# Attention and a two-layer MLP on one core: seven products for half of the first layer of four more token groups, and q and k of ten sets turned by a DMA

## The chip, the cores and the metric

The kernel runs on one core of one Trainium2 chip. The metric is the device time of one execution in microseconds; smaller is better. The kernel before takes 321.13 us, the median of three runs (320.48, 321.13 and 321.16).

## The reference: what is computed

Eight batches with eight heads, 576 positions of 64 elements per head, and 16 "beacon" positions ahead of the keys and values of each head. First causal attention (the beacons are seen by every query), then a two-layer MLP over the 4608 tokens of 512 elements, with an inner dimension of 2048. All inputs and the output are float32.

```python
k_all = concat([beacon_k, k], axis=2); v_all = concat([beacon_v, v], axis=2)   # 592 keys
scores = matmul(q, k_all^T) / sqrt(64);  scores above the diagonal (keys after the beacons) = -1e9
a = softmax(scores);  x = matmul(a, v_all) -> transposed to (4608, 512)
h = x @ w_in                       # 512 -> 2048
g = h * sigmoid(1.702 * h)
out = g @ w_out                    # 2048 -> 512
```

## The kernel before, in words

**Tiles and stages.** The work is done in float16 with sums in float32. Attention is cut into 16 *sets* of four heads of one batch (two sets per batch). Sets 0 to 3 are "early" and computed in finer pieces while the loads of the start come in. Scores are made transposed (keys on partitions, queries along the columns), with only the blocks below the diagonal: 1664 columns per head and set. From set 4 on these columns are laid end to end over all sets and cut into *chunks* of 512 columns; a chunk fills one score buffer `s` of four PSUM banks, one for each head, and can hold the end of one set and the beginning of the next. There are 55 chunks, numbered from 0; chunk 16 is the first of set 4. For each chunk PE computes the scores (`e_qk`, L506), ACT takes the exponential (`e_exp`, L518) into `E`, and POOL sets the part above the diagonal to zero (`e_mask`, L536). When a set is complete, DVE adds up pieces for the row sums (`e_zadd`, L554), PE multiplies by v (`e_av`, L594), and DVE inverts the row sums and writes the normalised result (`e_norm`, L628) into `xT`, a ring of 4 x 576 = 2304 tokens, in the layout that the MLP reads.

**How q and k come in.** POOL issues one DMA for q and one for k of each set (`e_load_qk`, L416), which casts to float16 and puts 18 consecutive positions of a head on one partition (long runs in DRAM). There are three buffers for each (`NB3` = 3). DVE then turns each of the two with a transpose of 32x32 blocks (`e_turn`, L472; for k also a small one for the beacons, L465, after a cast, L457, out of `bkf`, in which all sets' beacon keys lie). The result has 32 partitions for each head, and two elements of a head's 64 beside each other in a column, so that the scores of a piece take two matmuls of 32 rows (`d` = 0, 1) for each of four heads, the four heads in four row groups of the array. The turned q and k have two buffers each (`NB2` = 2): the turn of set s waits for the last scores of set s-2.

**The MLP.** The tokens are cut into groups: 0 and 1 have 256 tokens, 2 to 9 have 512. Numbers of groups here are the program's, from 0; the "token groups 4 to 7" of the change are 3 to 6. Groups 0 and 1 go a plain way. For groups 2 to 9 the second layer is done by seven products of half-sized blocks instead of eight (`products`, `e_prod`, L770), with sums of the activations before (`e_s`, L718, into three buffers `sA`), sums of w_out made once (`e_t`), and joins afterwards on DVE (`e_join`, L786, out of PSUM into `osb`, four buffers); SP stores the result (`e_store4`, L794). For groups 7, 8 and 9 (`FAST`) the first layer is done by seven products too: `fast` works in four *fours* of a group, each of two tiles of either half of the inner dimension; `e_part` (L864) does one product as four matmuls of 256 columns. ACT copies a partial result to another bank (`e_seed`, L874, two per four) and one product to SBUF (`e_keep7`, L883), DVE adds that back in (`e_sum7`, L886, two per four), and ACT applies the gelu (`e_gelu4`, L892). It needs four sums of the tokens per group (`e_xs`, L718 under `add`) and four sums of w_in (`e_ws`), which lie in q and k buffers that are no longer needed. For groups 2 to 6 the first layer is plain: 16 tiles of four matmuls with 512 columns (`e_m1`, L652), then gelu on ACT (`e_gelu`, L674). A group that crosses a multiple of 2304, which is group 5, has its 512 columns cut in two of 256.

**PSUM.** Eight banks: four (`RING`) for the MLP and the values, four for the score buffer. After the last chunk (`plan.breaks`) the score banks join the ring.

**ACT's tables.** Exponential and gelu need different tables; a change of table costs a table load, which the profile shows as ACT_TABLE_LOAD. Copies (`nc.scalar.mul`) need none.

**What sets the order.** The program first builds a list of operations with durations, due times and dependences (`Plan`, `op`), and places them on the engines in the order that the literal lists `ORDER` give for PE, ACT, DVE, POOL, Q (the landing of POOL's DMAs) and SP. The durations in the plan only serve to choose buffers and to merge the lists into one program; on the chip each engine runs its own list strictly in order and waits on semaphores.

Of the kernel before, what the change touches and what calls it, by code (L numbers as in the profile page):

```python
# [7 lines left out]
F16 = mybir.dt.float16  # L8
# [37 lines left out]
    ],  # L46
    "ACT": [
# [13 lines left out]
    ],  # L61
    "DVE": [
# [44 lines left out]
    ],  # L107
}


HELD = ("s", "zadd", "xsum", "wsum", "t", "mask", "bk")

# [1340 lines left out]
```

## Time and profile before

| | |
|---|---|
| median of three runs | 321.13 us (320.48 to 321.16) |
| span of the profiled execution, first to last instruction | 319.1 us |
| PE busy, of the span | 312.4 us (98%) |
| DVE busy | 246.5 us (77%) |
| ACT busy | 220.0 us (69%) |
| POOL busy | 113.2 us (35%) |
| bytes moved by DMA | 28.80 MB in 58379 packets, of which 41312 under 512 B |

The page names no other time of the profiled execution than its span. PE, DVE, ACT, POOL and SP are the engines; PEld is the loading of weights into the array, which overlaps with PE. L506 is line 506 of the kernel before; out<-in are names of the program's tiles. The shares of the page are averages over a start that waits for loads, a long middle and a short end; where a step matters, it is read from the stretch in which it lies.

### The profile page before, as it was taken

How to read it: one execution, taken by the hardware profiler on the slowest of the kernel's cores; microseconds unless marked ns; L12 is line 12 of the kernel's file. 1: busy time of each engine (PE TensorE's matmuls, PEld its weight loads, DVE VectorE, ACT ScalarE, POOL GpSimd, SP SyncE). 2: the span in 40 equal slices, each digit the busy share in tenths (PEclk: the TensorE clock that was granted, in tenths of full speed). 3: DMA queues.
4: the chain of work that ended last, by engine and by line, in shares of the span. 5: the costliest groups of instructions: out<-in, count | busy, mean ns of one | idle time of the engine just before them, and what ended most of it. 6: DMA issues, size and time to landing. Idle time of an engine off the chain costs nothing.

```text
span 319.1 us, 9554 instructions
## 1 busy us (share of the span) xinstructions
PE 312.4 (98%) x4119; PEld 223.9 (70%) x4119; DVE 246.5 (77%) x484; ACT 220.0 (69%) x275; POOL 113.2 (35%) x178
## 2 busy tenths in 40 slices
PE   6999999999999999999999999999999999999995
PEld 2567855544875467754778877646788888888884
DVE  4769966896797778875788979888978975684773
ACT  1777986557767686698867685778779786666520
POOL 8768488670238413472084108420420000000000
PEclk9999999999999999999999999999999999999999
DMA  7999999993109911398085707710021000011112
GB/s 122 175 202 209 206 192 185 170 228 65 37 2 165 208 26 37 46 153 123 7 81 90 115 2 81 100 35 2 2 83 51 4 20 15 33 69 36 67 68 99
DMA packets 58379, 28.80 MB, mean 90 GB/s; under 512 B 41312, under 2 KB 53728, under 8 KB 58336
## 3 DMA queue, kind: packets, MB, share of 16 engines
q0 software_dynamic: 47552, 18.49, 49.0%
q1 hardware_dynamic: 10576, 9.63, 9.3%
q8 instruction: 32, 0.52, 0.7%
q14 instruction: 11, 0.09, 0.1%
q10 hardware_dynamic: 208, 0.07, 0.1%
HBM read 37.22 MB, written 9.44 MB: 146 GB/s over the span
## 4 chain that ended last, share of the span: by engine, by line
PE 89%; DMA 5%; POOL 2%; ACT 1%; DVE 1%; issue 0%; DVEq 0%; POOLq 0%
PE u L770 31%; PE u L652 25%; PE u L864 12%; PE u L594 9%; PE s L506 8%; PE u L698 5%; DMA kn<-in_k_dram 3%; DMA qn<-in_q_dram 2%; POOL w L438 1%; ACT E L518 1%; ACT L674 0%; DVE kT L472 0%; POOL qn L416 0%; POOL kn L416 0%; ACT g L674 0%
## 5 line engine op out<-in xcount | busy, mean ns | idle before, releaser
L518 ACT ACTIVATE E<-s 128x2048 f16<-128x2048 f32 (+3 forms) x59 | 90.7, 1552 | 35.4 <-PE s L506 32.5
L652 PE MATMUL u<-xT,w 128*128 128x256 f16 (+1 forms) x512 | 87.9, 326 | 0.1
L536 POOL TENSOR_SCALAR_AFFINE_SELECT E<-E 128x512 f16<-128x512 f16 (+3 forms) x78 | 48.7, 643 | 89.6 <-ACT E L518 89.5
L652 PEld LDWEIGHTS <-w 128*128 128x128 f16 x512 | 49.2, 98 | 32.8 <-issue 1.1
L674 ACT ACTIVATE g<-u 128x512 f16<-128x512 f32 x80 | 43.6, 598 | 15.9 <-PE u L652 15.6
L770 PEld LDWEIGHTS <-g 128*128 128x128 f16 x512 | 48.4, 98 | 7.6 <-issue 0.5
L786 DVE SCALAR_TENSOR_TENSOR osb<-u,osb 128x512 f32<-128x512 f32 (+2 forms) x51 | 33.2, 654 | 21.5 <-PE u L770 16.3
L770 PE MATMUL u<-w,g 128*128 128x256 f16 x384 | 49.7, 273 | 0.0
L770 PEld LDWEIGHTS <-sA 128*128 128x128 f16 x384 | 36.6, 98 | 6.0 <-issue 0.8
L892 ACT ACTIVATE g<-u 128x512 f16<-128x512 f32 x48 | 27.2, 602 | 14.0 <-PE u L864 8.6
L506 PEld LDWEIGHTS <-kT 32*128 32x128 f16 x1088 | 22.4, 92 | 17.5 <-issue 10.8
L770 PE MATMUL u<-tB,sA 128*128 128x256 f16 x256 | 34.2, 273 | 0.0
L628 DVE TENSOR_TENSOR xT<-u,rz 128x352 f16<-128x352 f32 (+2 forms) x52 | 26.1, 521 | 8.4 <-PE u L594 7.7
L506 PE MATMUL s<-qT,kT 32*128 32x192 f16 (+14 forms) x992 | 30.9, 247 | 0.5 <-ACT E L518 0.3
L432 POOL DMA_DIRECT2D vb<-in_v_dram x32 | 27.8, 873 | 3.1 <-PE u L594 1.4
L594 PE MATMUL u<-E,vb 128*32 128x352 f16 (+8 forms) x928 | 27.7, 262 | 0.1
L594 PEld LDWEIGHTS <-vb 128*32 128x32 f16 (+1 forms) x928 | 20.1, 96 | 6.7 <-issue 2.9
L554 DVE TENSOR_TENSOR zs<-zs,E 128x1344 f16<-128x1344 f16 (+2 forms) x36 | 21.8, 605 | 0.9
L472 DVE STREAM_TRANSPOSE kT<-kn 128x576 f32<-128x576 f32 x16 | 20.1, 1256 | 2.7 <-DMA kn<-in_k_dram 2.2
L718 DVE TENSOR_TENSOR sA<-g 128x512 f16<-128x512 f16 x32 | 13.2, 417 | 10.9 <-ACT g L674 10.7
L472 DVE STREAM_TRANSPOSE qT<-qn 128x576 f32<-128x576 f32 x16 | 19.8, 1240 | 0.8 <-DMA qn<-in_q_dram 0.7
L864 PEld LDWEIGHTS <-w 128*128 128x128 f16 x192 | 18.7, 98 | 2.3
(76 smaller groups left out, 401.1 us busy)
## 6 DMA issues: line engine op xcount, KB each, us to landing
out_dram<-osb SPq DMA_DIRECT2D x35, 256.0 KB, 2.6
kn<-in_k_dram POOLq DMA_DIRECT2D x16, 288.0 KB, 6.8
qn<-in_q_dram POOLq DMA_DIRECT2D x16, 288.0 KB, 6.4
vb<-in_v_dram POOLq DMA_DIRECT2D x24, 128.0 KB, 6.8
w<-in_moe_w_in_dram POOLq DMA_DIRECT2D x8, 256.0 KB, 9.4
w<-in_moe_w_out_dram POOLq DMA_DIRECT2D x4, 512.0 KB, 12.1
vb<-in_v_dram POOLq DMA_DIRECT2D x8, 112.0 KB, 6.0
vb<-in_v_dram POOLq DMA_DIRECT2D x8, 80.0 KB, 6.8
```

The lines of the kernel that those rows point to most:

```text
L432: nc.gpsimd.dma_start(out=t[0 : hi - lo, j, h0:h1, :], in_=v[b, h0:h1, lo:hi, :].rearrange("h n d -> n h d"),)
L472: nc.vector.transpose(out=f32(dst.rearrange("p n e -> p (n e)")).rearrange("p (r t) -> p t r", t=TR), in_=f32(src[:, :]).rearrange("p (t c ...
L506: nc.tensor.matmul(u[:, o : o + w], kT[s % NB2][r : r + 32, j * P : (j + 1) * P, d], qT[s % NB2][r : r + 32, a : a + w, d], start=(d == 0) ...
L518: nc.scalar.activation(out=Es[s][:, h0:h1, c0:c1], in_=sall[(i, p)][:, :, o : o + c1 - c0], func=AFT.Exp, scale=0.125,)
L536: nc.gpsimd.affine_select(out=blk, in_=blk, compare_op=ALU.is_ge, fill=0.0, base=off + (Nb if j == 0 else 0), pattern=[[0, Q], [1, w]], ch ...
L594: nc.tensor.matmul(u[32 * h : 32 * h + 32, a:e], lhs, src[0:kw, h, col : col + e - a], start=first, stop=last, skip_group_check=s >= EARLY ...
L652: nc.tensor.matmul(u[:, o + a - t0 : o + e - t0], w1t[:, kp, nt * P : (nt + 1) * P], xT[:, kp, a % XR : (e - 1) % XR + 1], start=(kp == 0 ...
L674: nc.scalar.activation(out=gts[g][:, n0:n1, 0:w], in_=rings[("m1", g, n0)][:, 0 : n * w].rearrange("p (n w) -> p n w", n=n), func=AFT.Gelu ...
L770: nc.tensor.matmul(u[:, HM * mt : HM * (mt + 1)], lhs[:, n, mt * P : (mt + 1) * P], rhs[:, n, :], start=(n == 0 and (mt == 0 or apart) and ...
L786: nc.vector.scalar_tensor_tensor(out=osbs[(g, dst)][:, c0:c1], in0=rings[("p", g, p)][:, c0:c1], scalar=scale_of(g), in1=osbs[(g, src)][:, ...
L864: nc.tensor.matmul(u[:, HM * n : HM * (n + 1)], lhs[x][:, (2 * i + n) * P : (2 * i + n + 1) * P], rhs[:, x, :], start=fresh and n == 0 and ...
L892: nc.scalar.activation(out=gts[g][:, n : n + 2, HM * h : HM * (h + 1)], in_=rings[src][:, :].rearrange("p (n w) -> p n w", n=2), func=AFT. ...
```

## The change: what it does

1. **First layer.** `FAST` is now a table: groups 3 to 6 do the first two of their four fours by seven products and the other two plainly; groups 7 to 9 all four as before; group 2 none, but goes through the same function. For groups 2 to 6 the first layer is bound to a place after a given chunk (`PHASE`): there the four score banks join the ring, and the scores of the next chunk wait until all gelus of the group are done.
2. **Buffers for it.** The sums of w_in get tiles of their own (`SF`), the fourth sum of tokens as well (`ST[3]`); the kept product goes to four slots in the old q and k buffers, once sets 0 to 5 are turned. `sA` shrinks from three buffers to one: two of the sums are written over their inputs, and so wait for the product that reads these.
3. **Ring of tokens.** 2048 tokens instead of 2304. No group crosses its end any more; a normalised result that does is written in two instructions.
4. **q and k of sets 6 to 15.** POOL copies q, k and the beacons' k from DRAM to DRAM into scratch tensors with the cast to float16 (`e_stage`: rows of positions, four heads of 64 elements beside each other). SP then issues one transposing DMA for k and one for q (`e_xbar`) out of the scratch into the turned buffers, after the staging has landed and the scores two sets earlier are done. A head now lies on 64 partitions, and the scores of a piece are four matmuls of 64 rows in two row groups. Sets 0 to 5 keep the old way, with two load buffers instead of three, and `bkf` holds only their beacons.
5. **Order.** All lists of `ORDER` are new, and a list `BANK` gives the PSUM bank of each tile.

```diff
-    NE, NB2, NB3 = 3, 2, 3
+    NE, NB2, NB3 = 3, 2, 2
...
-    XR = 4 * S
+    XR = 2048
...
-    sA = [cst.tile([P, HN, HM], F16, tag=f"sA{i}", name=f"sA{i}") for i in range(3)]
+    sA = cst.tile([P, HN, HM], F16, tag="sA", name="sA")
+    SF = {i: cst.tile([P, 2, DFF // 2], F16, tag=f"SF{i}", name=f"SF{i}") for i in range(1, 5)}
...
-    bkf = cst.tile([P, NSET, D], F32, tag="bkf", name="bkf")
+    SQR = 3 * HS
+    bkf = cst.tile([P, SQR, D], F32, tag="bkf", name="bkf")
...
+    x7 = [f32(t[:, 0 : 2 * 512]) for t in qn + kn]
+    qD = [dr.tile([S, Q * D], F16, tag=f"qD{s}", name=f"qD{s}") for s in range(SQR, NSET)]
+    kD = [dr.tile([NK, Q * D], F16, tag=f"kD{s}", name=f"kD{s}") for s in range(SQR, NSET)]
+    qP, kP = ([t[:, :].rearrange("p (c n) -> p c n", c=2) for t in x] for x in (qTt, kTt))
...
+    def e_stage(s, which):
+        b, hs = divmod(s, HS)
+        hh = slice(Q * hs, Q * hs + Q)
+        if which == 2:
+            dst, src = kD[s - SQR][0:Nb, :], beacon_k[b, hh]
+        elif which:
+            dst, src = kD[s - SQR][Nb:NK, :], k[b, hh]
+        else:
+            dst, src = qD[s - SQR][:, :], q[b, hh]
+        nc.gpsimd.dma_start(out=dst.rearrange("n (h d) -> n h d", h=Q), in_=src.rearrange("h n d -> n h d"))
+
+    def e_xbar(s, which):
+        src, dst = ((qD, qP), (kD, kP))[which]
+        nc.sync.dma_start_transpose(out=dst[s % NB2][:, :, 0 : NK if which else S], in_=src[s - SQR][:, :])
...
+            if s >= SQR:
+                for h, u in heads.items():
+                    r = D * (h % 2)
+                    nc.tensor.matmul(
+                        u[:, o : o + w],
+                        kP[s % NB2][r : r + D, h // 2, j * P : (j + 1) * P],
+                        qP[s % NB2][r : r + D, h // 2, a : a + w],
+                        start=True,
+                        stop=True,
+                    )
+                continue
...
         if i == 0:
             add(eng, s1, a21, a22, ALU.add)
         elif i == 1:
-            add(eng, s2, s1, a11, ALU.subtract)
+            add(eng, a11, s1, a11, ALU.subtract)
         elif i == 2:
-            add(eng, s4, a12, s2, ALU.subtract)
+            add(eng, a12, a12, a11, ALU.subtract)
...
-    FAST = (7, 8, 9)
-    PHASE = {}
-    plan.breaks = sorted(set(PHASE.values())) + [len(CHUNKS) - 1]
+    FAST = {2: (), 3: (0, 1), 4: (0, 1), 5: (0, 1), 6: (0, 1), 7: (0, 1, 2, 3), 8: (0, 1, 2, 3), 9: (0, 1, 2, 3)}
+    PHASE = {2: 19, 3: 27, 4: 35, 5: 41, 6: 48}
+    plan.breaks = sorted(PHASE[g] for g in FAST if g in PHASE) + [len(CHUNKS) - 1]
...
+    XBAR = 1800
...
+            for which in (2, 1, 0) if s >= SQR else (1, 0):
+                if s >= SQR:
+                    staged[(s, which)] = pool_load(
+                        560 if which == 2 else 1300, 200 if which == 2 else 2000, [], lambda s=s, which=which: e_stage(s, which),
+                        name=f"st{s}.{which}.",
+                    )
...
     def turns(s):
+        if s >= SQR:
+            for which in (1, 0):
+                turn[(s, which)] = op(
+                    "SP", XBAR, [staged[(s, x)] for x in ((1, 2) if which else (0,))]
+                    + [qks[i] for i in CH_OF.get(s - NB2, [])], lambda which=which: e_xbar(s, which), name=f"xbar{s}.{which}.",
+                )
+            return
...
         for i in range(HN // 2):
-            tiles(i)
+            (tiles if i in FAST[g] else plain)(i)
```

In the plan a transposing DMA holds SP for 1.8 us (`XBAR`) and lands 4.5 us after that; a staging holds POOL for 1.3 us.

More of the change, by code (lines that the diff above doesn't have):

```diff
@@ L180, in opening @@
                 if None not in ends:
-                    open_at.append((max([0] + [x + 60 for x in ends]), i))
+                    open_at.append((max([since] + [x + 60 for x in ends]), key not in self.partial, i))
             return min(open_at, default=None)
@@ L236, in lat @@
             return {"bk0": 2500, "bk1": 5200}.get(o.name, 9000)
+        if d.name[:5] == "store":
+            return 2600 if o.eng != "SP" else 0
+        if d.name[:4] == "xbar":
+            return 4500 if o.eng != "SP" else 0
         if d.eng == "Q" and d.name[:4] in ("ldqk", "ldv1", "ldv2", "ldv3", "ldv4", "ldv5", "ldv6", "ldv7"):
@@ L256, with f32 @@
     nc = tc.nc
+    def f32(ap):
+        return ap.bitcast(F32)
     B, H, S, D = q.shape
@@ L837, in e_xs @@
         if not ST:
-            for n in (1, 2, 4):
+            for n in range(1, 5):
                 t = sp.tile([P, 512], F16, tag="sig", name="sig")
@@ L859, in e_part @@
             6: (SF[2], ST.get(2)),
-            7: (SF[3], tokens(g, 0, 1)),
+            7: (SF[3], ST.get(3)),
         }[p]
@@ L878, in e_keep7 @@
     def e_keep7(g, i, src, slot):
[L879 to L882 removed]
+        p7s[(g, i)] = x7[slot]
         nc.scalar.mul(out=p7s[(g, i)], in_=rings[src][:, :], mul=1.0)
@@ L936, in load_v @@
         )
+    staged = {}
     def load_batch(b):
         for s in range(HS * b, HS * b + HS):
-            for which in (1, 0):
-                load_qk(s, which, max(0, due_of(s) - 22000))
+            for which in (2, 1, 0) if s >= SQR else (1, 0):
[4 more added lines that the diff above has]
+                    )
+                else:
+                    load_qk(s, which, max(0, due_of(s) - 22000))
         for j in range(-1, NJ):
@@ L1064, in values @@
             else:
+                split = 65 if (b * S + q0) // XR != (b * S + q1 - 1) // XR else 0
                 norms[(s, half, x)] = op(
-                    "DVE", 65 + 1.045 * cols * (2 if whole and half == 0 else 1), [avs[(s, x, half)], z2[0 if whole else half]],
+                    "DVE", 65 + split + 1.045 * cols * (2 if whole and half == 0 else 1), [avs[(s, x, half)], z2[0 if whole else half]],
                     lambda x=x, half=half: e_norm(s, x, half),
@@ L1115, in weights, with sums @@
             tds[i] = prev[0]
[L1117 removed]
+    tds, ends, fives = {}, {}, {}
     def products(g):
[L1120 removed]
+        eng = "DVE"
         sd = {}
[L1122 to L1131 removed]
+        def sums(i, deps):
+            for n0 in range(0, HN, SQ):
+                n1 = n0 + SQ
+                o = op(
+                    eng, 336, deps(n0) + [x for n in range(n0, n1) for x in gates[(g, n)] + gates[(g, n + HN)]],
+                    lambda n0=n0, n1=n1: e_s(g, i, n0, n1, eng), pr=2, name=f"s{g}.{i}.{n0}",
+                )
                 sd[(i, n0)] = o
+        sums(0, lambda n0: fives.get(g - 1, []))
+        sums(3, lambda n0: [sd[(0, n0)]])
         lhs = {1: None, 2: None, 3: 2, 4: None, 5: 0, 6: 1, 7: 3}
+        made = {}
         rhs = {1: None, 2: None, 3: None, 4: 2, 5: 0, 6: 1, 7: 3}
@@ L1214, in products @@
         store(c12, "m", 0, 1)
-        ends[g] = [c11, c21, c12]
-    wsum, xsums, held, readers, closing = {}, {}, {}, {}, {}
+    wsum, xsums, held, readers, closing, first, used = {}, {}, {}, {}, {}, [], {}
     def fast(g, xs, old):
         ph = plan.breaks.index(PHASE.get(g, len(CHUNKS) - 1))
-        if not wsum:
-            both = lambda s: [turn[(s, 0)], turn[(s, 1)]]
-            free = {
-                1: both(NSET - 3), 2: both(NSET - 2), 4: [bkc[NSET - 1]],
-                3: [x for n in range(g) for x in m1s[n]],
-            }
+        if not wsum and FAST[g]:
+            free = {}
+            loads = [x for n in w1_of for x in w1_of[n]]
             prev = None
             for i in (1, 2, 4, 3):
-                prev = wsum[i] = op("DVE", 1250, free[i] + [prev], lambda i=i: e_ws(i), name="wsum")
-        free = readers.get(g - 1, [])
+                prev = wsum[i] = op("DVE", 1250, free.get(i, []) + loads + [prev], lambda i=i: e_ws(i), name="wsum")
+        free = [x for n in range(g) for x in readers.get(n, [])] + list(gated)
         xsum, prev = {}, None
-        for i in (1, 2, 4, 3):
+        for i in (1, 2, 4, 3) if FAST[g] else ():
             prev = xsum[i] = op("DVE", 336, free + xs + [prev], lambda i=i: e_xs(g, i), name=f"xsum{g}")
+            m1s.setdefault(g, []).append(prev)
         lhs = {3: 4, 5: 1, 6: 2, 7: 3}
-        fixed = g not in PHASE
         def tiles(i):
@@ L1242, in tiles @@
             k = len(held)
-            slot = k % 2 if fixed else None
-            last = []
-            if fixed:
-                last = held.get(k - 2) or [turn[(NSET - 1, w)] for w in range(2)]
+            slot = k % (2 * NB3)
+            last = used.get(slot, [turn[(s, w)] for s in range(SQR) for w in range(2)])
             def part(p, at, deps, fresh=False):
-                deps = list(deps) + xs + old
+                deps = list(deps) + xs
                 if p in lhs:
@@ L1290, in tiles, with plain @@
             gelu(1, 0, a2, "b")
-            held[k] = [a1, a2]
+            held[k] = used[slot] = [a1, a2]
+        def plain(i):
+            for n in (2 * i, 2 * i + 1, HN + 2 * i, HN + 2 * i + 1):
+                key = ("m1", g, n)
+                plan.phase[key] = ph
+                if GROUPS[g][0] // XR != (GROUPS[g][1] - 1) // XR:
+                    plan.partial.add(key)
+                pe = op(
+                    "PE", 4 * (512 / 2.4 + 2.8), xs + w1_of[n], lambda n=n: e_m1(g, n, n + 1), kind="m1", ring=key, mode="m",
+                    name=f"m1.{g}.{n}",
+                )
+                m1s.setdefault(g, []).append(pe)
+                o = op(
+                    "ACT", 490, [pe] + old, lambda n=n: e_gelu(g, n, n + 1), closes=key, name=f"gelu{g}.{n}.", table="g",
+                )
+                closing.setdefault(ph, []).append(o)
+                gates[(g, n)] = [o]
         for i in range(HN // 2):
-            tiles(i)
+            (tiles if i in FAST[g] else plain)(i)
     def mlp(g):
```

102 lines of the change are left out of this document (50 added, 52 removed), and 175 rows, old and new, of tables (BANK, ORDER).

## The prediction

> **What bounds the kernel now.** I read the busy line first, then the table of windows, then the chain, and last ACT's timeline.
>
> ```profile
> span 319.1 us, 9554 instructions
> ...
> PE 312.4 (98%) x4119; PEld 223.9 (70%) x4119; DVE 246.5 (77%) x484; ACT 220.0 (69%) x275; POOL 113.2 (35%) x178
> ```
>
> A PE that is busy 98% of the span says little alone, so the next view asks where the other 6.7 us lie.
>
> ```profile
> 26.00:67.00 41.00, 40.91 (x655) 25.98 (x653) 33.65 (x62) 29.77 (x32) 30.10 (x46) 1.00 1.41 195
> 64.00:72.00 8.00, 8.00 (x39) 3.64 (x38) 7.24 (x9) 4.55 (x9) 6.03 (x9) 1.00 1.75 226
> 67.00:104.00 37.00, 37.00 (x502) 23.37 (x501) 29.19 (x53) 26.75 (x29) 13.96 (x23) 1.00 0.58 90
> 104.00:141.00 37.00, 36.91 (x478) 23.07 (x480) 29.19 (x57) 27.77 (x33) 15.35 (x25) 1.00 0.60 85
> 141.00:173.00 32.00, 32.00 (x433) 21.86 (x422) 24.82 (x48) 25.40 (x27) 12.23 (x18) 1.00 0.69 89
> 173.00:206.00 33.00, 33.00 (x495) 26.52 (x494) 28.32 (x56) 22.79 (x26) 12.61 (x19) 1.00 0.56 69
> 206.00:240.00 34.00, 34.00 (x432) 22.70 (x431) 28.90 (x54) 25.94 (x31) 9.07 (x13) 1.00 0.11 38
> 240.00:304.00 64.00, 64.00 (x690) 56.58 (x689) 47.05 (x98) 44.49 (x84) 0.00 (x0) 1.00 0.10 36
> 304.00:319.00 15.00, 11.61 (x107) 10.17 (x104) 8.14 (x20) 1.05 (x2) 0.00 (x0) 1.00 0.24 83
> ```
>
> The columns are length, PE, PEld, DVE, ACT and POOL busy, granted clock, DMA share, GB/s. From 67 to 304 PE has no hole and the clock is 1.00 throughout: only less PE work, or work done in fewer cycles, shortens this stretch. The pace of that work stands in the chain (start, length, line, matmuls).
>
> ```profile
> 67.40 11.22 PE u L652 x52
> ...
> 173.04 11.44 PE u L652 x104
> 184.48 0.56 PE s L506 x8
> ...
> 303.82 11.80 PE u L770 x108
> ```
>
> A 128x512 matmul of the first layer costs 11.22/52 = 0.2158 us, one of 256 columns 11.80/108 = 0.1093 (11.44/104 = 0.110 at L652). A chunk of scores costs 0.56.
>
> There is a second limit just under the first one. While attention runs, ACT and PE hand a single score buffer to and fro:
>
> ```profile
> 122.36 1.88 ACT L518 ACTIVATE E<-s 128x2048 f16<-128x2048 f32 x1 [0.94 <-PE s L506]
> 125.08 1.88 ACT L518 ACTIVATE E<-s 128x2048 f16<-128x2048 f32 x1 [0.83 <-PE s L506]
> ...
> 136.24 1.28 ACT L674 ACT_TABLE_LOAD   x1
> ...
> 140.72 1.28 ACT L518 ACT_TABLE_LOAD   x1
> 142.01 1.02 ACT L518 ACTIVATE E<-s 128x1024 f16<-128x1024 f32 x1
> 143.06 1.28 ACT L674 ACT_TABLE_LOAD   x1
> ...
> 153.16 1.02 ACT L518 ACTIVATE E<-s 128x1024 f16<-128x1024 f32 x1
> ...
> 206.48 1.28 ACT L674 ACT_TABLE_LOAD   x1
> ...
> 220.89 1.88 ACT L518 ACTIVATE E<-s 128x2048 f16<-128x2048 f32 x1
> ...
> 239.24 1.28 ACT L892 ACT_TABLE_LOAD   x1
> ```
>
> One chunk takes 1.88 + about 0.95, say 2.85 us, and a block of gelus with a table load at each end stands between some chunks. Groups 7 to 9 get ACT only when this chain has ended (239.24), and PE then has some 76 us of work left (304 - 239.2 = 64.8, and 11.6 behind). So a saving ahead of 239 counts only if the score chain gets shorter too.
>
> **The change, part by part.** *First layer of groups 3 to 6* (the fourth to the seventh). Two tiles of each half of the inner dimension, a four, were 16 matmuls of 512, 16 x 0.2158 = 3.453 us; by seven products it is 28 of 256, 28 x 0.1093 = 3.060. Two such fours per group, four groups: 8 x 0.393 = 3.14 us off PE. *The ring of tokens* goes from 2304 to 2048, so group 5 is no longer cut in two: 128 x 0.110 = 14.08 becomes 64 x 0.2158 = 13.81, 0.27 off. PE falls by 3.4 us. *The sums for the second layer* are now written over their inputs, so the one for product 6 waits for product 1; between them lies product 2, 16 x 0.1093 = 1.75 us, which covers a sum of about 0.47 (a row below). I cost that at nothing; without the cover it would be 0.47 in each of eight groups. The four weight sums only move to an earlier place.
>
> *What that adds on ACT and DVE.*
>
> ```profile
> L874 ACT ACTIVATE u<-u 128x512 f32<-128x512 f32 x24 | 14.0, 594 | 3.8 <-PE u L864 2.8 <-DVE osb L786 0.9
> L886 DVE TENSOR_TENSOR u<-u,qn 128x512 f32<-128x512 f32 x12 | 8.0, 695 | 4.5 <-PE u L864 3.6 <-ACT qn L883 0.9
> L718 DVE TENSOR_TENSOR sig<-xT,sig 128x512 f16<-128x512 f16 x6 | 2.8, 473 | 0.1
> L472 DVE STREAM_TRANSPOSE kT<-kn 128x576 f32<-128x576 f32 x16 | 20.1, 1256 | 2.7 <-DMA kn<-in_k_dram 2.2
> L465 DVE STREAM_TRANSPOSE kT<-bkn 128x32 f32<-128x32 f32 x16 | 3.1, 193 | 0.1
> L457 DVE CAST bkn<-bkf 128x64 f16<-128x64 f32 x16 | 3.9, 243 | 0.8 <-DMA bkf<-in_beacon_k_dram 0.8
> L628 DVE TENSOR_TENSOR xT<-u,rz 128x352 f16<-128x352 f32 x24 | 12.5, 520 | 5.2 <-PE u L594 4.9
> ```
>
> Each of the 8 fours gets two seeds and one kept product on ACT, 24 x 0.594 = 14.3 us, and two sums on DVE, 16 x 0.695 = 11.1; each group four token sums, 16 x 0.473 = 7.6. The sets that cross token 2048 or 4096 write some normalised outputs in two pieces, at most a dozen more of 0.520, 6 us. DVE loses 20 turns x 1.256 = 25.1 and 10 x (0.193 + 0.243) = 4.4. DVE ends 5 us lighter, hidden by a PE without holes; ACT ends 14.3 heavier. The seeds need no table, and fit the 0.8 to 0.95 us in which ACT waits for a chunk. The worst case is that all lengthen the chain: 14.3 us, less what the gelu blocks have idle.
>
> *The gelu blocks.* The new wait holds the next chunk's scores until the group's gelus are done, so a block is whole. Today group 4's is cut by one exponential and a pair of table loads (136.24 to 143.06), 2 x 1.28 = 2.6 us of chain. The longest run without a hole is this:
>
> ```profile
> 181.03 3.22 ACT L674 ACTIVATE g<-u 128x512 f16<-128x512 f32 x6 [0.28 <-PE u L652]
> ```
>
> 0.537 per gelu. A block of 22 ACT steps is then 22 x 0.537 + 2.57 = 14.4 us; with 16 of them inside and the seeds in the gaps outside, 11.2. Today's take from 14.4 (206.48 to 220.89) to 16.9 (136.24 to 153.16). So the chain loses 2.6 to some 10 us, or gains 3 if each of 22 costs its full 0.6; I take a loss above PE's 3.4, which leaves PE as the limit.
>
> *Scores of sets 6 to 15.* Today eight matmuls of 32 rows do a piece, four at once in two rounds; afterwards four of 64 rows, two at once, also two rounds. The row of 0.56 for one piece of 512 is two rounds of 512 columns and 0.13 of switching. I take no change; ends: 32.5 chunks x 0.13 = 4.2 saved, or, if two halves of the array don't run side by side, two more rounds, 32.5 x 0.43 = 14.0 lost.
>
> *The path of q and k.* No transposing DMA stands in this trace.
>
> ```profile
> L432 POOL DMA_DIRECT2D vb<-in_v_dram x32 | 27.8, 873 | 3.1 <-PE u L594 1.4 <-DMA w<-in_moe_w_out_dram 0.7 <-DMA qn<-in_q_dram 0.5
> L416 POOL DMA_DIRECT2D kn<-in_k_dram x16 | 9.2, 575 | 9.0 <-DVE kT L472 3.8 <-DVE bkn L457 2.6 <-DVE zt L604 0.8
> ...
> DMA to landing us min/median/max: 4.0/6.8/10.8
> ```
>
> ```profile
> L794 SPq DMA_DIRECT2D out_dram<-osb x31: 372/372/789, 85.1 to 314.6; - x31
> ```
>
> ```profile
> q0 software_dynamic: 4832, 0.61, 68.1%
> ...
> out_dram<-osb SPq DMA_DIRECT2D x35, 256.0 KB, 2.6
> ```
>
> The landing row is that of kn; the q0 row is the window 191 to 205, v loads alone. The turn of a set may begin when the scores two sets earlier are through PE, and must be there three or four chunks later. Counting 1664 columns a set in chunks of 512, with blocks after chunks 27, 35, 41 and 48, only sets 7, 10 and 14 have three chunks and no block between: 3 x 2.85 - 0.56 = 8.0 us. Set 9 has four, 10.8; the others have a block more. Into 8.0 must fit k's issue, q's issue and a landing. Ends: 0.37 + 0.37 + 2.6 = 3.3 (a store's issue and landing) and, with the plan's 1.8 per issue and kn's longest, 14.4. The plan itself holds 1.8 + 1.8 + 4.5 = 8.1. I take it, since a transposed piece of 303 KB is nearest in size to the 256 KB store and starts with all data at hand: a few tenths in three places, 0.4 us in all.
>
> The Trainium skill, DMA: Bandwidth & Descriptors, "Latency and other measured facts", puts a transposing DMA at 261 GB/s when the middle dimension isn't contiguous, and "Anatomy of one DMA" a fixed 2 us; an estimate from it is 303 KB / 261 GB/s + 2 = 3.2 us to land, by which none of the three sets waits and the sum would be 0.4 lower. No row here shows it.
>
> *Queues.* POOL: 20 loads of 0.575 go; 20 stagings and 10 short ones come, each longer than a v load's 0.873 for 1024 runs (2304 runs: between 0.87 and 2.0). That is 12 to 35 us on an engine busy 113 of 319; masks wait up to 2 us behind one, and values and sums wait for those, while PE has products to do. SP: an xbar waiting for scores holds the stores behind it, these hold osb, and that the joins on DVE; SP does little else. The first 72 us, in which the DMA share is 1.41 and 1.75, also get the staging of the first sets, and sets 4 and 5 now wait for the buffers two sets back. *DMA engines:* 0.681 x 14 us / 4832 = 1.97 ns of all 16 per run; a staging of 2304 is 4.5 us, twenty 91. Share x length from 67 to 206 is 0.58 x 37 + 0.60 x 37 + 0.69 x 32 + 0.56 x 33 = 84 us of 139; the rows reach 1.75, so room is there, but landings will lengthen.
>
> The same skill page, "Specifications", wants 512 B or more in a run, and says that below it the engine reads, modifies and writes; here runs go from 256 B to 128 B. By that a staging could cost more than the same runs of v into SBUF; no run here shows it, and it is what feeds the second rival.
>
> **Sum.** The page gives no other time of the profiled execution than its span of 319.1; the runs' median of 321.13 is 2.0 above it, taken as unchanged. 321.13 - 3.4 + 0.4 = 318.1; span 316.1.
>
> **Rivals.** *1, no gain:* the blocks become ACT-bound and eat what PE saves, so that 239 stays where it is; for it speaks that ACT goes from 220 to 234 and the 0.6 per step where ACT waits between; against it, seeds that fit gaps and the table pair that goes. 321.1. *2, slower:* turned q and k come late in the three sets with 8.0 us. PE's order is written out, so all behind waits. With kn's median landing, 1.8 + 1.8 + 6.8 = 10.4, 2.4 late, three times: 7.2 and 318.1 + 7.2 = 325.3; with 14.4, (3 x 6.4 + 3.6) = 22.8 and 341. It decides from 8.0 us between the scores and the landing. For it: the small runs. Against: DMA shares of 0.56 to 0.69 in this stretch, and stagings that wait for no buffer. *3, rounds of 64 rows don't overlap:* 318.1 + 14.0 = 332. *4, scores cheaper:* 318.1 - 4.2 = 313.9. *5, the DMA doesn't turn in one go* but in 2-byte pieces: 592 x 256 runs of 1.97 ns are 300 us a turn and the time is in the thousands; that a single instruction is used speaks against it.
>
> **How the numbers follow.** Forecast 0.53, its own range 316.5 to 320.3. Rival 1 0.10; rival 2 0.26; 3 and 5 together 0.05; 4 0.06. The measurement can tell 0.2%, 0.64 us, from no change. Faster: 0.53 + 0.06 + 0.01 of rival 1 = 0.60; the same: 0.09; slower: 0.31. The range goes from 316 to 326.5: it leaves out rival 4 (0.06), 3 and 5 (0.05) and the upper 0.09 of rival 2.
>
> **What would show it.** Right: 560 matmuls of 256 columns at L864's successor instead of 336 (20 fours of 28 against 12), PE busy near 309 and still without holes from 67 to 300; one pair of table loads fewer; PE waits for kT and qT under 1 us. Wrong: PE holes ahead of the first chunk of sets 7, 10 and 14 (rival 2); gelu blocks above 15 us and a later last exponential (rival 1); a chunk of scores other than 0.56 (3, 4). The prediction fails as a whole if PE waits for staging from DRAM, or if the first 72 us get longer because their DMA traffic grows.

## The result: slower by 2.7%, and the profile after

| | before | after |
|---|---|---|
| median of the runs shown together | 321.02 us (320.48 to 321.16) | 329.69 us (327.87 to 330.58) |
| ratio, 95% interval | | 1.0268 [1.0238, 1.0299] |
| span of the profiled execution | 319.1 us | 328.1 us |

The kernel is 8.7 us slower, where 3.0 us faster was forecast. From the page of after: the busy line, the packets, and the two kinds of DMA queue (packets, MB, share of 16 engines).

```profile
span 328.1 us, 9027 instructions
...
PE 312.1 (95%) x3835; PEld 228.3 (70%) x3835; DVE 242.9 (74%) x481; ACT 227.7 (69%) x297; POOL 139.3 (42%) x188
...
DMA packets 125993, 34.67 MB, mean 106 GB/s; under 512 B 111488, under 2 KB 123904, under 8 KB 125952
...
q0 software_dynamic: 91872, 18.57, 66.0%
```

PE now has 16.0 us without work (328.1 - 312.1) where it had 6.7; the packets have doubled. The view of what PE waited for (engine, line, releaser: us in all, times, longest) names the largest hole, and PE's own timeline says where it lies:

```profile
PE s L557 <- DMA kT<-kD: 4.1, 1, 4.1
...
PE u L923 <- DVE sig L784: 1.5, 1, 1.5
PE u L923 <- DVE u L942: 1.0, 2, 0.5
PE u L656 <- DVE osb L852: 0.8, 1, 0.8
```

```profile
125.77 0.60 PE L557 MATMUL s<-qT,kT 64*128 64x512 f16 x4 [4.09 <-DMA kT<-kD]
```

That is the first chunk of set 8, which waits for its turned k. Windows around it (the last three columns are granted clock, DMA share, GB/s):

```profile
106.00:114.00 8.00, 7.39 (x49) 4.50 (x47) 4.39 (x6) 7.07 (x15) 8.00 (x11) 1.00 1.60 168
114.00:122.00 8.00, 7.68 (x75) 5.41 (x73) 7.56 (x19) 6.54 (x9) 7.46 (x9) 1.00 2.12 188
122.00:130.00 8.00, 4.23 (x24) 2.80 (x24) 3.24 (x6) 1.88 (x1) 0.94 (x2) 0.79 2.08 155
```

POOL is full, the DMA share is above 2, and the clock falls to 0.79 of full speed behind the hole. What is in flight there is told by the DMA view of 100 to 128 us (last column: median us from the start of the issue to landing) and by the timelines of POOL and SP:

```profile
qD<-in_q_dram POOLq DMA_DIRECT2D x5, 288.0 KB, 13.7
out_dram<-osb SPq DMA_DIRECT2D x4, 256.0 KB, 7.5
kD<-in_k_dram POOLq DMA_DIRECT2D x3, 288.0 KB, 13.7
```

The two transposing DMAs of set 8 by themselves (the DMA view of 106 to 107 and of 117 to 118 us):

```profile
qT<-qD SPq DMA_TRANSPOSE x1, 8.9
kT<-kD SPq DMA_TRANSPOSE x1, 8.4
```

The issue on POOL, then SP:

```profile
105.48 2.68 POOL L486 DMA_DIRECT2D kD<-in_k_dram  x1
```

```profile
106.27 2.98 SPq L490 DMA_TRANSPOSE qT<-qD  x1
109.30 1.09 SPq L860 DMA_DIRECT2D out_dram<-osb  x2
117.35 2.18 SPq L490 DMA_TRANSPOSE kT<-kD  x1
```

Eight stagings of q and k (issued from 98.6 to 114.0 us) are in flight in this stretch and take 13.7 us to land. The k of set 8 is staged among them at 105.5 and lands 11.9 us later, so SP's transposing DMA for it can start only at 117.4, and its data come at 125.7. The other seven are of later sets, four of them of sets 12, 14 and 15, whose transposing DMAs are issued from 176 us on.

### The profile page after: what moved, and what is told of

Its sections match the earlier page's. It is cut to its first block, busy times and chain, and to the rows that moved or that the text cites. A ratio compares the mean times of both kernels' runs of the same rounds, so it can differ in the third digit from the quotient of the medians.

```text
span 328.1 us, 9027 instructions
## 1 busy us (share of the span) xinstructions
PE 312.1 (95%) x3835; PEld 228.3 (70%) x3835; DVE 242.9 (74%) x481; ACT 227.7 (69%) x297; POOL 139.3 (42%) x188
## 5 line engine op out<-in xcount | busy, mean ns | idle before, releaser
L836 PEld LDWEIGHTS <-g 128*128 128x128 f16 x768 | 74.0, 99 | 13.2 <-issue 1.5
L718 PE MATMUL u<-xT,w 128*128 128x512 f16 (+1 forms) x320 | 60.1, 337 | 0.1
L852 DVE SCALAR_TENSOR_TENSOR osb<-u,osb 128x512 f32<-128x512 f32 (+2 forms) x51 | 33.1, 654 | 20.7 <-PE u L836 19.6
L472 POOL DMA_DIRECT2D vb<-in_v_dram x32 | 38.2, 1330 | 11.7 <-PE u L656 11.7
L923 PEld LDWEIGHTS <-SF 128*128 128x128 f16 x320 | 31.0, 98 | 9.5 <-issue 3.5
L836 PE MATMUL u<-tB,g 128*128 128x256 f16 x256 | 36.3, 280 | 0.0
L923 PE MATMUL u<-sig,SF 128*128 128x256 f16 x240 | 34.2, 273 | 1.5 <-DVE sig L784 1.5
L694 DVE TENSOR_TENSOR xT<-u,rz 128x352 f16<-128x352 f32 (+6 forms) x58 | 26.7, 489 | 5.2 <-PE u L656 4.7
L933 ACT ACTIVATE u<-u 128x512 f32<-128x512 f32 x40 | 23.4, 590 | 8.6 <-PE u L923 4.5
L784 DVE TENSOR_TENSOR g<-g 128x512 f16<-128x512 f16 x64 | 27.9, 452 | 1.7 <-PE u L836 1.1
L486 POOL DMA_DIRECT2D kD<-in_k_dram x10 | 24.8, 2476 | 0.3 <-issue 0.3
L923 PE MATMUL u<-xT,w 128*128 128x256 f16 x160 | 23.7, 272 | 0.3 <-ACT u L933 0.3
```

The source lines that it names most:

```text
L472: nc.gpsimd.dma_start(out=t[0 : hi - lo, j, h0:h1, :], in_=v[b, h0:h1, lo:hi, :].rearrange("h n d -> n h d"),)
L694: nc.vector.tensor_tensor(out=xT[:, 2 * hs + x : 2 * hs + x + n, at : at + c1 - c0], in0=rings[("av", s, x, half)][:, 0 : n * w].rearrange ...
L718: nc.tensor.matmul(u[:, o + a - t0 : o + e - t0], w1t[:, kp, nt * P : (nt + 1) * P], xT[:, kp, a % XR : (e - 1) % XR + 1], start=(kp == 0 ...
L784: (nc.vector if eng == "DVE" else nc.gpsimd).tensor_tensor(out=out, in0=a, in1=b, op=op)
L836: nc.tensor.matmul(u[:, HM * mt : HM * (mt + 1)], lhs[:, n, mt * P : (mt + 1) * P], rhs[:, n, :], start=(n == 0 and (mt == 0 or apart) and ...
L852: nc.vector.scalar_tensor_tensor(out=osbs[(g, dst)][:, c0:c1], in0=rings[("p", g, p)][:, c0:c1], scalar=scale_of(g), in1=osbs[(g, src)][:, ...
```

## Experiments

After the result I held **theory A**: the staging is late, because it is bunched on POOL and in the DMA queue. Its rivals: **B**, the undivided gelu blocks and the added steps of the seven-product halves cost the time; **C**, the transposing DMAs themselves do. Numbers in the lists are the program's operations: 756 is the staging of k of set 8, 764 q of 9, 818 k of 10, 826 and 824 q and k of 11, 1127 and 1129 k and q of 12, 1133 and 1135 k and q of 13, 1189 and 1191 of 14, 1195 and 1197 of 15.

### First four: take the staging apart

**e1**, POOL's order only (the list of the landings, Q, follows it):

```diff
-    470, 1133, 472, 770, 768, 1129, 816, 610, 774, 455, 826, 776, 453, 628, 756, 1197, 599, 1189, 608, 602, 772, 764, 609, 1191, 818, 1131,
+    470, 756, 472, 770, 768, 764, 816, 610, 774, 455, 818, 776, 453, 628, 826, 599, 608, 602, 772, 609, 1131,
...
-    845, 782, 970,
+    845, 782, 1129, 1133, 970,
...
-    1004, 1003, 1156,
+    1004, 1003, 1189, 1191, 1197, 1156,
```

> Only the order of GpSimd's queue is changed: k of set 8, q of 9 and k of 10 are staged earlier, and the stagings of sets 11 to 15 that nobody needs before 160 us are moved out of the stretch from 104 to 130 us. Theory A (staging is late: GpSimd's queue and the DMA queue back up where the stagings are bunched): the 4.1 us hole of TensorE at 125.8 us and the half clock behind it (1.7 us) go, and some of the late masks: 322 to 324 us. Theory B (the blocks of the fast halves on ScalarE and TensorE cost it) and theory C (the transposing DMAs themselves cost it): 329 to 330 us.

**e2**, long runs (the scratch holds another arrangement):

```diff
-        nc.gpsimd.dma_start(out=dst.rearrange("n (h d) -> n h d", h=Q), in_=src.rearrange("h n d -> n h d"))
+        nc.gpsimd.dma_start(
+            out=dst.rearrange("n c -> (n c)").rearrange("(p x) -> p x", p=P),
+            in_=src.rearrange("h (r t) d -> (h r) (t d)", t=TR),
+        )
```

(the beacons' small staging stays).

> The staging of q and k moves the same bytes with the same cast into the same scratch, in 128 runs instead of 2304, so that the scratch holds them in another arrangement (this leaves out the turn into one row per position; the scores are of other numbers). Everything else as after. Theory A: GpSimd's hold falls from 1.6 us to about 0.6 and the landings to 2 or 3 us, the holes go, masks are back at 0.65 us: 318 to 321 us. Theories B and C: 329 to 330 us.

**e3**, no staging but that of set 6:

```diff
     def e_stage(s, which):
+        if s > SQR:
+            return
...
-        nc.sync.dma_start_transpose(out=dst[s % NB2][:, :, 0 : NK if which else S], in_=src[s - SQR][:, :])
+        nc.sync.dma_start_transpose(out=dst[s % NB2][:, :, 0 : NK if which else S], in_=src[0][:, :])
```

> Only set 6 is staged; the transposing DMAs of the other nine sets read set 6's scratch, so they and the fast halves run as after, and 27 of the 30 stagings are left out (the scores of nine sets are of set 6's q and k). Theory A: all lateness goes: 316.5 to 319 us, 318.4 being the time before (321.0) less the 2.6 us by which the written schedule of after is shorter. Theories B and C: 329 to 330 us.

**e4**, no transposing DMA from set 8 on:

```diff
     def e_xbar(s, which):
+        if s >= SQR + NB2:
+            return
```

> All staging is kept; the transposing DMAs of sets 8 to 15 are left out, so that these sets' scores use the q and k of sets 6 and 7 and wait for no DMA. Theory A: the hole at set 8 (4.1 us and 1.7 at half clock) goes, the masks that are late behind the stagings stay: 322 to 325 us. Theory C: 317 to 319 us. Theory B: 329 to 330 us.

| run | median us | ratio to before [95%] |
|---|---|---|
| e1, other order | 330.50 | 1.0310 [1.0282, 1.0337] |
| e2, long runs | 331.78 | 1.0345 [1.0312, 1.0379] |
| e3, no staging | 322.33 | 1.0041 [1.0028, 1.0055] |
| e4, no transposing | 325.46 | 1.0153 [1.0127, 1.0178] |

e3 settles the first question: all transposing DMAs and all halves run, and 7.4 of the 8.7 us are gone. B falls as a cause of these, and so does C by itself. But A as I had it missed: e3 and e4 end above what it gave them (316.5 to 319 and 322 to 325), and e1 and e2 far above. The two large misses show what it lacked. In **e1** set 8 is served in time, and the hole has moved to set 12 (PE's waits, then POOL, then SP):

```profile
PE s L553 <- DMA qT<-qD: 5.2, 1, 5.2
```

```profile
145.90 1.64 POOL L482 DMA_DIRECT2D qD<-in_q_dram  x1
...
176.83 1.59 POOL L482 DMA_DIRECT2D kD<-in_k_dram  x1
177.92 3.75 POOL L482 DMA_DIRECT2D qD<-in_q_dram  x2
```

```profile
180.16 6.76 SPq L486 DMA_TRANSPOSE qT<-qD  x2
```

The scratch of set 12 had been filled long before; its q is the first row of POOL. What is late is the transposing DMA itself: three stagings that I had moved to 177 us are in flight beside it. In **e2** POOL's hold has gone, and the hole has doubled (POOL's group, PE's waits, SP, the two transposing DMAs of set 8 in the DMA view, a window):

```profile
L489 POOL DMA_DIRECT2D kD<-in_k_dram x10 | 5.1, 513 | 1.5 <-DMA vb<-in_v_dram 1.5
```

```profile
PE s L563 <- DMA kT<-kD: 8.6, 1, 8.6
```

```profile
105.00 6.75 SPq L496 DMA_TRANSPOSE qT<-qD  x1
111.81 1.14 SPq L866 DMA_DIRECT2D out_dram<-osb  x2
113.04 11.81 SPq L496 DMA_TRANSPOSE kT<-kD  x1
```

```profile
qT<-qD SPq DMA_TRANSPOSE x1, 20.7
kT<-kD SPq DMA_TRANSPOSE x1, 15.1
```

```profile
122.00:130.00 8.00, 1.83 (x9) 0.76 (x10) 1.05 (x3) 0.70 (x1) 0.00 (x0) 0.50 1.05 180
```

The same two landings without staging, from e3's DMA view, and SP's issue of the second:

```profile
qT<-qD SPq DMA_TRANSPOSE x1, 4.3
kT<-kD SPq DMA_TRANSPOSE x1, 5.6
```

```profile
108.19 2.08 SPq L492 DMA_TRANSPOSE kT<-kD  x1
```

So the number of runs is not what makes them late. In e2 the staging of k of set 8 is in time (issued at 103.5, landed 6.6 us later), but its transposing DMA holds SP for 11.8 us and lands 15.1 after the start of its issue instead of 5.6. The eight stagings follow each other more closely there (97.4 to 109.2 us, against 98.6 to 114.0 in after). In after itself two parts add up: against e3 the transposing DMA of k starts 9.2 us later (117.35 against 108.19), since its staging has not landed, and it lands after 8.4 us instead of 5.6. I split theory A: **A1**, the many short runs cost; **A2**, a transposing DMA that shares the DMA engines with several stagings is late, whatever their runs. Against both stands **D**, that the staged bytes cost their time wherever they are put.

### Next four: keep them apart

**e5**, POOL's order only:

```diff
-    1187, 820, 762, 461, 420, 758, 395, 447, 413, 406, 421,
+    1187, 461, 420, 395, 447, 413, 406, 758, 421,
...
-    1193, 437, 760, 440, 471, 470, 1133, 472, 770, 768, 1129, 816,
+    1193, 756, 437, 760, 762, 440, 471, 470, 472, 764, 820, 818, 770, 768, 816,
...
-    632, 631, 785,
+    632, 631, 826, 824, 785,
...
-    845, 782, 970, 973, 1195, 1139,
+    845, 782, 1127, 1133, 1135, 1129, 1189, 970, 1191, 973, 1195, 1197, 1139,
```

(758 and 820 are q of 8 and 10, 762 k of 9; the moved ones are gone from their old places.)

> Order of GpSimd's queue alone, 16 of the 20 stagings of q and k moved: k of 8, k of 9 behind 78 us, q of 9, q and k of 10 at 88 to 92, q and k of 11 at 120, those of 12 to 15 between 143 and 160 us, so that none is in flight beside the transposing DMAs of sets 8, 9, 12, 13, 14 and 15 and few beside the loads of v. Theory A2 (runs e1 and e2 left of theory A only this: a transposing DMA that shares the DMA engines with several stagings is late, whatever their runs are): as without staging, 322.3 us, within 321.5 to 323.5. Theory D (the staged bytes cost their time wherever they are put): 326 to 330 us.

**e6**, and SP's last stores:

```diff
-    1640, 1622, 1650, 1654, 1646,
+    1640, 1622, 1646, 1650, 1654,
```

> As the kernel with the stagings apart, and one store of the last group is issued ahead of two others on SyncE. In the run without staging the program ends 4.6 us behind TensorE's last matmul, 3.5 before. Expected 0.3 to 1.0 us less than with the stagings apart alone: 321 to 322.5 us by theory A2, 325 to 330 by D.

**e7** is e5 with e2's edit, **e8** is e4 with e2's edit.

> The stagings apart, and moved in 128 long runs (the scratch holds another arrangement, so the scores are of other numbers). Theory A2: the same as with the stagings apart, within 0.7 us: once nothing collides, the length of the runs is worth only GpSimd's shorter hold. Theory A1 (the many short runs are what costs): 1.5 us or more below it.

> The transposing DMAs of sets 8 to 15 left out as in e4 (325.5 us), and the staging in long runs as in e2. What e4 keeps over no staging at all (322.3 us) is 3.1 us. If that is GpSimd's 1.6 us hold of every staging, which makes masks late: 322 to 323 us. If it is the DMA engines' time (late loads of v): 325 to 326 us.

| run | median us | ratio to before [95%] |
|---|---|---|
| e5, apart | 322.18 | 1.0047 [1.0032, 1.0062] |
| e6, and last store | 321.80 | 1.0038 [1.0023, 1.0053] |
| e7, apart, long runs | 322.47 | 1.0053 [1.0036, 1.0069] |
| e8, no transposing, long runs | 321.82 | 1.0037 [1.0024, 1.0051] |

**e5 is the answer to the 7.5 us**: with every byte still staged and the kernel changed in nothing but the place of 15 DMAs (the expectation says 16; one of them, 1195, keeps its place), the time is that of no staging at all. A2 holds, D falls. It takes away both parts at once, the late staging and the slow landing; what each is worth alone is not shown, nor at which shared place the transposing DMA is held up. The two landings of set 8, and the hold of SP by all ten transposing DMAs of q (ns, least/median/most):

```profile
qT<-qD SPq DMA_TRANSPOSE x1, 5.0
kT<-kD SPq DMA_TRANSPOSE x1, 5.3
```

```profile
L486 SPq DMA_TRANSPOSE qT<-qD x10: 1246/1330/2428, 64.7 to 209.7; - x10
```

e7 gains nothing, so A1 falls once the stagings are apart. One of its five executions, the profiled one, took 325.8 us: there the transposing DMA of k of set 7 (issued at 88.4 us) met three stagings (issued from 88.7 on) and landed after 8.7 us, and PE waited 2.6 us for it. But e4 and e8 show that A1 had a part where they are bunched. With the transposing DMAs out of the way, e4 keeps 3.1 us over e3, and the long runs of e8 take it away. The row of the masks on POOL, of e4 and of e8 (x78, then busy us and mean ns), says how:

```profile
L600 POOL TENSOR_SCALAR_AFFINE_SELECT E<-E 128x512 f16<-128x512 f16 (+3 forms) x78 | 66.4, 1008 | 87.0 <-ACT E L582 64.5 <-issue 20.4 <-DVE zs L618 2.1
```

```profile
L606 POOL TENSOR_SCALAR_AFFINE_SELECT E<-E 128x512 f16<-128x512 f16 (+3 forms) x78 | 48.7, 644 | 103.3 <-ACT E L588 72.1 <-issue 20.7 <-DVE g L792 8.2
```

A mask behind a queue of stagings ends later (1.01 us instead of 0.64), and the sums on DVE wait for it (DVE's waits, of e4 and of e8):

```profile
DVE zs L618 <- POOL E L600: 8.5, 3, 5.6
```

```profile
DVE zs L624 <- POOL E L606: 3.5, 1, 3.5
```

PE then waits longer for DVE (1.6 us for `sig` in e4, 0.7 in e8), and in neither view for v. So by the medians the 7.4 us between after and e3 are 4.2 for turned q and k (329.7 - 325.5, the hole and the half clock) and 3.1 for POOL. The split is rough: these kernels did not all run on one chip, and the spans of the profiled executions (328.1, 322.5 and 319.9) give 5.6 and 2.6.

### The rest: where the gain of the halves is

e5 and e6 are still 0.4% slower than before, though PE has less to do. **Theory E**: small waits of PE for DVE, which another order takes away. **F**: the halves gain nothing by themselves. **G**: a four is worth its 0.393 us. Two attempts with a new order for all engines, searched with the program's own schedule, came first. **e9** is e6 so ordered; **e10** also has groups 3 to 6 plain:

```diff
-    FAST = {2: (), 3: (0, 1), 4: (0, 1), 5: (0, 1), 6: (0, 1), 7: (0, 1, 2, 3), 8: (0, 1, 2, 3), 9: (0, 1, 2, 3)}
+    FAST = {2: (), 3: (), 4: (), 5: (), 6: (), 7: (0, 1, 2, 3), 8: (0, 1, 2, 3), 9: (0, 1, 2, 3)}
```

> The kernel with the stagings apart and the last store moved, with the order within the queues of TensorE, ScalarE, VectorE and GpSimd searched again, in the kernel's own schedule with the sums of the tokens put at 0.45 us instead of 0.34 (0.555 and 0.485 us for two kinds of them in the traces) and a staging at 1.6 us of GpSimd. The schedule ends 1.45 us earlier than that of the kernel with the stagings apart with the same costs. Theory E (what is left over the time before are small waits of TensorE for VectorE, 0.4 to 0.7 us each, that the order can take away): 320.0 to 321.0 us, level with before. Theory F (the halves carry a cost that no order hides): 321.5 to 322.5 us.

> As e9, but token groups 3 to 6 computed plainly throughout (no seven-product scheme there; the staging and the transposing DMAs stay), its order searched in the same way. By the schedules it ends 2.8 us later than e9. If the halves are worth what the prediction said (3.4 us of TensorE): 2.5 to 3.5 us above e9. If they are worth nothing (theory F): within 1 us of e9.

Both missed: 326.04 us (1.0173 [1.0151, 1.0195]) and 340.51 us (1.0605 [1.0581, 1.0629]). They say nothing on the halves. The schedule knows a staging as a fixed time and no sharing, so the search undid what e5 had put in order: e9's masks are back at 0.91 us (e6: 0.72), and in e10 the transposing DMAs meet stagings again: four stagings are issued from 178.0 to 181.8 us, two transposing DMAs of q follow at 186.3, hold SP for 8.0 us together and land after 10.8 (median of the two). PE's waits:

```profile
PE s L539 <- DMA qT<-qD: 8.9, 1, 8.9
```

From there on I changed single instructions. The longest waits of PE for DVE in e6, behind the start, are these (`sig` holds sums of the tokens, `osb` joined results, `zs` below row sums):

```profile
PE u L919 <- DVE sig L780: 0.7, 1, 0.7
PE u L652 <- DVE osb L848: 0.5, 1, 0.5
PE u L652 <- DVE xT L690: 0.4, 1, 0.4
PE u L919 <- DVE u L938: 0.4, 1, 0.4
```

**e11** moves three instructions in DVE's list (797 is a sum of set 8, 357 a join of group 2, 990 a norm of set 10):

```diff
-    797, 647, 589, 648, 649, 650, 595,
+    647, 589, 648, 649, 650, 595, 797,
...
-    475, 476, 357,
+    357, 475, 476,
...
-    944, 990,
+    990, 944,
```

> As e6 (321.8 us), with three instructions of VectorE moved a few places in its queue, at the places where TensorE waited for it there: a sum of set 8 behind the sums of the tokens of group 4 (wait of 0.68 us), a join of group 2 ahead of two sums of set 5 (0.50), a norm of set 10 ahead of a join of group 5 (0.45). Theory E (the rest over before is such waits): 320.2 to 321.3 us, about 1 us below e6. Theory F (the halves carry a cost that the order cannot take away): 321.6 to 322.2 us. After e9 missed, only these three places are touched.

**e12** is e6 with `3: ()` and `5: ()` in `FAST`, and the steps of these halves out of the lists.

> As e6, but token groups 3 and 5 computed plainly throughout, with every other instruction in e6's order. If a four by the scheme is worth the 0.393 us of the prediction, the four fours undone cost 1.6 us: 323.4 us, within 322.9 to 323.9 (the kernel's schedule says 1.62). Theory F: 321.5 to 322.2 us, or below.

e11: 321.20 us, 1.0005 [0.9996, 1.0014], level with before: three instructions gave 1 us by the ratios, as E said, with 0.6 us of uncertainty. The traces show half of it: the waits for `osb` and `xT` at L652 are gone and that for `sig` has shrunk to 0.3, but a new one of 0.7 for `zs` has come, and PE's idle time from 60 to 220 us falls from 2.6 to 2.0. e12: 322.18 us, 1.0037 [1.0023, 1.0051], the ratio of e6: undoing four of the eight fours cost nothing, against 1.6 us by G. Four more runs on one chip, beside 35 of before, tell the groups apart:

> The kernel of e11 once more, so that the three next to it are compared on one chip: 321.2 us, 1.000 to 1.001 of the time before.

> e11 with token group 3 computed plainly. Theory G (a four is worth its 0.393 us wherever TensorE does not wait): 0.8 us above e13. Theory F (in group 3 TensorE waits for VectorE and gets nothing): 0 to 0.2 us above e13.

> e11 with token group 5 computed plainly. Theory G: 0.8 us above e13. Theory F for all halves: 0 to 0.2 us above e13.

> e11 with groups 3 and 5 computed plainly. Theory G: 1.6 us above e13. Theory F: within 0.4 us of e13, as e12 stood to e6 (ratios to before of 1.0037 and 1.0038, each within 0.0015, from two chips).

| run | median us | ratio to before [95%] |
|---|---|---|
| e13, e11 again | 320.95 | 1.0005 [0.9996, 1.0014] |
| e14, group 3 plain | 320.79 | 1.0003 [0.9991, 1.0015] |
| e15, group 5 plain | 322.12 | 1.0035 [1.0024, 1.0047] |
| e16, both plain | 321.74 | 1.0025 [1.0016, 1.0035] |

Group 5's two fours are worth 1.0 us by the ratios ((1.0035 - 1.0005) x 321), G's 0.8 within the interval. Group 3's are worth nothing, with 0.5 us either way. Both together are worth 0.6 us (e16 less e13), less than G's 1.6. The profiled execution of e14 runs 1.4 us later than that of e13 from the first layer of group 2 on (63.11 against 61.71), so group 3 is compared over the same work, from the first matmul of its first layer to the next product of a second layer behind it (length, then PE, PEld and DVE busy), of e13 and of e14:

```profile
97.13:115.24 18.11, 17.72 (x135) 11.77 (x133) 14.13 (x24) 15.50 (x24) 9.54 (x15) 1.00 1.08 138
```

```profile
98.53:116.70 18.17, 18.17 (x111) 9.47 (x109) 10.36 (x16) 13.24 (x18) 10.77 (x15) 1.00 1.09 138
```

Of the 0.79 us that the two fours should save, 0.06 is left in the length. With the halves DVE has 3.8 us more to do in this stretch, and PE stands still for 0.39, done plainly not at all. The other 0.3 of the loss lies in time that the profile counts as busy; what it is was not traced. Groups 4 and 6 were not tried alone. No version ran faster than before.

## Why the prediction was wrong, point by point

- **The step that failed** is the one on queues: "so room is there, but landings will lengthen", which has no term in the sum; the only time for landings is 0.4 us in three tight sets. The mean DMA share was no measure of it. What counts is what is in flight in the few microseconds of a transposing DMA, and that follows from where POOL's list puts the stagings. Measured: 7.5 us (after less e5; 7.1 by the ratios).
- **Rival 2 had the kind right and the place wrong.** Turned k came late, once, in set 8, which had a gelu block's room more than sets 7, 10 and 14; for these three no wait of PE is listed. The 8.0 us between scores and landing did not decide; the staging ahead of it did, which the prediction held against this rival ("stagings that wait for no buffer"). Its 325.3 us also lacked POOL's part (3.1 us by e3 and e4) and the half clock behind the hole. With both it would have come near the 329.7.
- **A staging's hold of POOL** was bounded by 0.87 and 2.0 us, and is 1.6 alone (the row of 1.59 in e1). Where stagings and masks follow each other their rows overlap, and the page of after gives 2.5 and 2.7 us as means for k and q. The masks behind it were foreseen ("up to 2 us") but given no time of their own, under the cover that "PE has products to do". That cover was not there: 3.1 us.
- **The path of a transposing DMA by itself** was taken too long, not too short. The 8.1 us (1.8 + 1.8 + 4.5) that the plan holds for q and k of a set are 4.7 for set 9 in e3 (q issued at 116.37, k at 117.69 and landed 3.4 us later), and all twenty landings of e3 take 3.2 to 6.7 us from the start of their issue, 4.2 in the median. The estimate of 3.2 us that the prediction works out from the Trainium skill, DMA: Bandwidth & Descriptors, "Latency and other measured facts" and "Anatomy of one DMA", is 1.0 below this median; the fixed 2 us in it stand there for DMAs that GpSimd issues, and these are issued by SP.
- **PE's work, 3.4 us off, was right as work.** The filler matmuls that keep PE busy in the first stage vary and must be taken out first; their rows, of before and of e3:

```profile
L1416 PE MATMUL u<-tB 128*128 128x512 f32 (+3 forms) x23 | 10.3, 562 | 2.6 <-DVE tB L327 2.6
```

```profile
L1512 PE MATMUL u<-tB 128*128 128x512 f32 (+3 forms) x27 | 11.7, 554 | 2.6 <-DVE tB L367 2.6
```

```profile
PE 310.0 (97%) x3835; PEld 227.3 (71%) x3835; DVE 240.1 (75%) x481; ACT 227.7 (71%) x297; POOL 105.3 (33%) x161
```

  312.4 - 10.3 = 302.1 before, 310.0 - 11.7 = 298.3 in e3, 3.8 less. As time nothing of it is left even in e13, whose span is 319.0 us against 319.1; its page, and the windows of before and of e13 (length, PE busy):

```profile
PE 309.8 (97%) x3835; PEld 227.4 (71%) x3835; DVE 240.3 (75%) x481; ACT 227.7 (71%) x297; POOL 139.5 (44%) x188
```

```profile
60.00:260.00 200.00, 199.91 (x2693) 138.20 (x2686) 165.85 (x314) 148.91 (x177) 69.47 (x103) 1.00 0.49 73
```

```profile
60.00:260.00 200.00, 197.95 (x2384) 141.62 (x2383) 158.11 (x305) 157.81 (x202) 97.78 (x118) 1.00 1.02 108
```

  Of the 3.6 us less work in e13 (its filler is 11.3 us), 2.0 became idle time between 60 and 260 us, 1.0 went into more filler, and 0.5 into idle time ahead of 60 and behind 260.
- **"DVE ends 5 us lighter, hidden by a PE without holes" failed by place.** DVE is 6.4 us lighter (246.5 to 240.1), but the sums stand just ahead of the products that need them, and PE waited 0.3 to 0.7 us in several spots. e11 moved three instructions and is 1 us below e6, of which its trace shows 0.6.
- **Rival 1 had the time of the mended order, but not its cause.** Its 321.1 us are what e11 and e13 take (321.2 and 320.95), and "239 stays where it is": the last exponential starts at 235.8 before and at 235.7 in e13. But PE's listed waits for ACT are 0.3 us in both; what eats the saving stands in the two points above.
- **Rivals 3 to 5** gained no support: a chunk of scores takes PE 0.53 to 0.56 us from its first matmul to the next instruction (e13, 118 to 140 us) where it took 0.56 to 0.58 before (100 to 125 us), and rivals 3 and 4 needed 0.99 or 0.43.
- **Not foreseen:** one store more at the very end. From PE's last matmul to the end are 319.1 - 315.6 = 3.5 us before and 319.9 - 315.3 = 4.6 in e3:

```profile
313.70 1.91 PE L770 MATMUL u<-w,sA 128*128 128x256 f16 x16
```

```profile
313.80 1.47 PE L838 MATMUL u<-w,g 128*128 128x256 f16 x12
```

  e6 moved it and is 0.4 us below e5, within the uncertainty.
- **Left open:** what the start costs. Sets 0 to 3 with two load buffers instead of three waited for a turn in some executions (1.6 us in the profiled one of e14, none in that of e13).

## What to carry to other kernels

Cost a new DMA stream by what else is in flight at the moment when its result is due, not by the mean share, and look first at where the issuing queue bunches it: here the order of 15 issues was worth 7.5 us, and longer runs nothing once these stood apart. Work that is off the critical path "on balance" must be checked at the instruction that waits for it. Do not let a schedule that has no model of a shared resource choose the order on it.

## What the runs showed of the hardware

- A transposing DMA of some 300 KB landed 3.2 to 6.7 us after the start of its issue with next to no staging (e3). Beside eight short-run stagings it took 8.4 and 8.9 (set 8 of after), beside as many with long runs 15.1 and 20.7 (e2), and its issue then held SP for up to 11.8 us instead of 1.3. The Trainium skill, DMA: Bandwidth & Descriptors, "Queues, rings and completion order", says that each engine goes round its rings packet by packet; that the longer packets made it later agrees with this, but no run here looked at single packets.
- POOL's cost of a DMA follows the runs: 1.59 us for 2304 (alone, e1), 0.51 for 128 of the same bytes (e2). It does not follow that the shorter one helps: e2 was the slowest of the first four, though the masks of e8 gain by it.
- The granted clock fell to 0.50 over the 8 us around e2's hole of 8.6 us, and 0.79 around the hole of 4.1 in after. The Trainium skill, TensorE: Matmul & The Clock Gate, "Part 1", gives half rate after an idle window of about 3.4 us; both holes are longer, and the trace agrees.
